# A layer norm, a long convolution and a feed-forward block on one core: x enters by (x - mean)(1 + rstd y) + mean, first writers write plainly, more transposes go by DMA, scales and first roots move to ScalarE

## The chip, the cores and the metric

The kernel runs on one core of a Trainium2 chip. The metric is the device time in microseconds, the median of several executions; lower is better. Separate executions of the kernel before lie between 1259.02 and 1259.97 us.

## What is computed

`x` has 2048 rows and 1024 columns, fp32. It is normalized by rows; the normalized rows gate a long causal convolution of `k` and `v`, and feed a feed-forward block of width 3584. Both results are added to `x`.

```python
def _A_ref(q, k, v, shift_k, ssm_k, ssm_D):      # q: the normalized x
    ...                                          # k_shift: four taps along the rows
    kv = k_shift * v
    kv_f, kf_f = rfft(kv, 2 * S), rfft(ssm_k, 2 * S)
    y = irfft(kv_f * kf_f)[:S] + kv * ssm_D
    return q * y

def _B_ref(x, w1, w2):
    return silu(x @ w1) @ w2

xn = (x - mean) / sqrt(var + 1e-5)
return x + _A_ref(xn, ...) + _B_ref(xn, B_w1, B_w2)
```

## The kernel before

One program issues all instructions in an order that a planner works out. Each piece of work is a generator that yields operations (`Op`: engine, estimated busy time, memory read and written) or conditions to wait for. `Order.run` keeps a clock for each engine and emits, again and again, the operation whose estimated start less its stream's bias is the earliest. Each engine then executes its own instructions strictly in the emitted order, and waits by semaphores where data or a buffer is not ready. `L` is a plain DMA issued from SyncE (SP), `X` a transposing DMA of 2-byte data from SP, `G` an accumulating DMA from GpSimd (POOL), `V`, `A` and `T` are VectorE, ScalarE and TensorE operations. Many operations pass through the same helpers: L348 and L351 (VectorE), L359 (ScalarE), L335, L341 and L345 (DMAs).

**Feed-forward.** Products are made of three fp16 matmuls (high and low parts), so each factor is split into a high part (ScalarE) and a low part (VectorE) with a scale that is a power of two. The scale comes from a sum of squares: `norm` adds it over partitions by a matmul with ones, and a chain on VectorE (reduce, a bound from below, two shifts that leave the exponent, then scalings by `then`) leaves it in `wsc` for the 14 column pairs of `w1`. `units` computes the first product by Strassen's seven products, on four PSUM banks `ff` that ScalarE and VectorE evacuate; `feed_forward` then computes the second product for the plain part of the width, row block by row block and half by half of the columns (`result`, ScalarE, scale `invc`), and `units2` the Strassen part. The hidden layer goes through device memory; its blocks come back into the twelve half buffers of `wo`. The parts of `w2` are split in `norms_w2`, in places that the first product leaves.

**Layer norm.** `ln_rows` takes rows in groups of 2, 2, 4 and 8 blocks: statistics on VectorE (two on ScalarE), then for each group a chain of eleven small VectorE instructions for the inverse root (L506 to L516), then the application to the rows (L528 on VectorE or ScalarE).

**Convolution.** Eight groups `g` of 128 channels, each in four steps `t`. `gate` makes k times v; its sums of squares give the group's scales in `csc` through `norm`. `signal_parts` transposes the signal and splits it: for `g < BY_DMA` (3) four TensorE transposes into a PSUM tile `py` and a split from there; for the other groups a split into the single buffer `cm` and two DMA transposes. `stage1`, `forward`, `product`, `inverse` and `stage1_inv` make the transform, the product and the inverse; `result_scales` makes the last scale by `norm` again. `norm_rows` loads x a second time in pieces `xg` and normalizes them on ScalarE; `gated` multiplies them by the convolution's result on VectorE (scalar `sc[:, 5:6]`) and adds them to `out` by POOL.

**Output.** `copies` first copies x to `out` by 16 DMAs of 512 KB on SP (L1161); everything else is added to it by accumulating DMAs on POOL: 64 half row blocks of the feed-forward and its Strassen part, and 64 pieces of the convolution. Only the very last piece is read back, added and written plainly.

Of the kernel before, what the change touches and what calls it, by code (L numbers as in the profile page):

```python
# [38 lines left out]
BY_DMA = 3  # L39
# [6 lines left out]
APPLY = (4, 5, 6, 7)  # L46
GUESS = 0x5f3759df
# [69 lines left out]
class Order:  # L117
# [4 lines left out]
    def __init__(self):  # L122
        self.free = defaultdict(float)
        self.wrote, self.read = {}, {}
        self.slots, self.patterns = {}, {}
        self.streams = []
        self.pipe = self.now = 0.0
        self.table = AF.Silu
# [171 lines left out]
def h3_ffn_kernel(ctx, tc, x, kp, vs, fs, shift, dskip, w1, w2, cfwd, cinv, out):  # L300
# [53 lines left out]
    def a_act(o, i, func, scale=1.0, bias=None, total=None):  # L354
        def f():
            kw = {} if bias is None else {"bias": bias}
            if total is not None:
                kw["accum_out"] = total
            nc.scalar.activation(o, i, func, scale=scale, **kw)  # L359
        ins = [i] + [s for s in (scale, bias) if s is not None and not isinstance(s, float)]  # L360
        p = A(f, o, ins)
        p.table = func if func == AF.Silu else None
# [22 lines left out]
    nmr = cst.tile([P, NT], F32, name="nmr")  # L385
    rstd = cst.tile([P, NT], F32, name="rstd")
# [9 lines left out]
    invc = cst.tile([P, 1], F32, name="invc")  # L396
    one = cst.tile([P, 1], F32, name="one")
# [40 lines left out]
    def norm(ring, ss, ns, then, flags, margin=1.5):  # L438
# [4 lines left out]
        e, etok = pw.tile([P, 2])  # L443
# [22 lines left out]
        for t in flags[1]:  # L466
            t.set()
# [11 lines left out]
    def ln_rows():  # L479
        for t0, n, bias in ((0, 2, 0.26), (2, 2, 0.17), (4, 4, LB), (8, 8, 0.03)):  # L480
# [36 lines left out]
            p = V(chain, r, [ag[:, 0:n]], us=1.8)  # L517
            p.writes += [e, f, v]
            yield p
            for k, t in enumerate(order_in):  # L520
                xt = xts[t][0]
                if k == (0 if t in APPLY else 1):
                    yield V(lambda: nc.vector.scalar_tensor_tensor(nmr[:, q], mean, -1.0, r, op0=MUL, op1=MUL), nmr[:, q], [ag[:, 0:n], r], us=0.2)
                if t in APPLY:
# [137 lines left out]
    def scales_w1():  # L662
        for n, (_, i) in enumerate(pairs):
# [19 lines left out]
            yield from norm(ctxs["nm"], ss[:, 0:m], (m,), then, ([wsc[:, i]], [flag["scaled", n], tok]))  # L683
# [288 lines left out]
    def feed_forward():  # L972
# [13 lines left out]
        for h in range(2):  # L986
            for ts in TOGETHER[h]:
                pos = {}
                for c in range(NC):
                    for t in ts:  # L990
# [11 lines left out]
                        if c == NC - 1:  # L1002
                            add(result(h, t, *pos[t]), EB)
                            flag["half"].set()
# [123 lines left out]
    flag["copied", 0] = Token(NT // 2)  # L1128
    flag["copied", 1] = Token(NT // 2)
    flag["conv out"] = Token(NG * 4 * 2)  # L1130

    def result(h, t, po, tok):
# [21 lines left out]

    def copies():
        for a in range(NT):
            yield flag["unit", a // 2] if a < NT // 2 else flag["half"]
            n = NT // 2
            q = slice(a % n * 2 * P, (a % n + 1) * 2 * P), slice(a // n * W, (a // n + 1) * W)
            o = out[q]  # L1160
            yield Op("SP", 0.4, 0.1, lambda: nc.sync.dma_start(o, x[q]), [], [], 0.3, P * D * 4)  # L1161
            flag["copied", a // n].set()
# [95 lines left out]
    def load_w2():  # L1258
        rings = ctxs["wraw"], ctxs["w2n"]
        for h, j in [(h, j) for h in range(2) for j in PLAIN[::2]]:  # L1260
            yield lambda: any(r.pairs() for r in rings)
            raw, tok = next(r for r in rings if r.pairs()).pair([P, 2, W])
            yield L(raw, w2r[:, j:j + 2, h * W:(h + 1) * W])
# [27 lines left out]
    def convolution(floor):  # L1291
# [19 lines left out]
        def rest(floor):  # L1311
# [8 lines left out]
            add(copies(), 0.0)  # L1320
# [28 lines left out]
        def gate():  # L1349

            for g in range(NG):
                yield csc_r.ready
                scs[g] = sc, _ = csc_r.tile([P, 8])
# [30 lines left out]
                def then(e):  # L1384
                    nc.vector.reciprocal(sc[:, 0:2], e)
                    nc.vector.tensor_scalar(sc[:, 0:2], sc[:, 0:2], 2.0 ** (15 - 64), None, op0=MUL)
                    nc.vector.tensor_scalar(sc[:, 2:4], e, 2.0 ** 64, None, op0=MUL)
                yield from norm(py_r, ss[:, 0:6], (4, 2), then, ([sc[:, 0:4]], [flag["scales", g]]), 4.0)
# [170 lines left out]
        def result_scales(g):  # L1559
# [4 lines left out]
            def then(e):  # L1564
                nc.vector.reciprocal(sc[:, 4:5], e)
                nc.vector.tensor_scalar(sc[:, 4:5], sc[:, 4:5], 2.0 ** (15 - 64 - 50), None, op0=MUL)
                nc.vector.scalar_tensor_tensor(sc[:, 5:6], e, 2.0 ** (64 - 41), sc[:, 2:3], op0=MUL, op1=MUL)
                nc.vector.tensor_tensor(sc[:, 5:6], sc[:, 5:6], sc[:, 3:4], op=MUL)
            yield from norm(py_r, ss[:, 8:12], (4,), then, ([sc[:, 4:6]], [flag["un", g], sss[g][1]]), 3.0)
# [54 lines left out]
        def norm_rows():  # L1624

            for g in range(NG):
                for t in TO:
# [33 lines left out]
        def gated(g, t, py, tok):  # L1661
# [4 lines left out]
            yield v_stt(flat[1], flat[0], sc[:, 5:6], flat[1], MUL, MUL)  # L1666
            tok.set()
            if t == TO[-1]:
                stok.set()
            yield flag["copied", g // (NG // 2)]  # L1670
            for b in range(2):
                yield G(out4[b][:, :, t, g * P:(g + 1) * P], xg[:, b])
                xtok.set()
                flag["conv out"].set()

# [24 lines left out]
    def more_rows():  # L1700
        for t in (8, 9, 12, 13, 10, 11, 14, 15):
            yield from load_row(t)
        yield L(taps, shift)
        yield L(cfw, cfwd)
        yield L(civ, cinv)

# [18 lines left out]
    nc.scalar.activation(warm, ones[:, 0:1], AF.Silu)  # L1725
# [56 lines left out]
```

## Time and profile before

| | before |
|---|---|
| median (lowest to highest of 3) | 1259.5 us (1259.02 to 1259.97) |
| profiled execution, its time | 1259.29 us |
| profiled execution, its span | 1257.5 us |
| mean granted TensorE clock | 0.996 |
| DMA, mean rate | 228 GB/s |

The profile shows one execution, instruction by instruction. A row of a group gives the line, engine and operation, what is written and read, the shapes and the count; then the busy time, the mean duration in ns, and the idle time of the engine just before these instructions with what ended it. A row of the timeline gives the start, the duration, the engine (PE is TensorE, PEld its weight loads, DVE VectorE, ACT ScalarE, POOL GpSimd; a q behind a name means its sequencer). A row of a window gives its length, the busy time of PE, PEld, DVE, ACT and POOL with the count of instructions, the granted clock, the busy share of the DMA engines and their GB/s. A row of waits gives who waited for whom, the sum in us, how often, and the longest. Matmuls are pipelined: their durations overlap, and their pitch is read from the starts.

### The profile page before, as it was taken

Reading aid. Unit: us, or ns where it says so; the run is one execution under the profiler, and the core shown is the slowest. Engines: PE = TensorE matmul, PEld = TensorE weight load, DVE = VectorE, ACT = ScalarE, POOL = GpSimd, SP = SyncE. Lnnn points to the kernel's source line nnn. Section 1 sums busy time; section 2 is a strip of 40 time slices with the busy share of each in tenths; the row PEclk is TensorE's granted clock in tenths of the full one; section 3 lists DMA queues with packets and bytes.
Section 4 is the critical chain, followed back from the end, with each engine's and each line's share of the span. In section 5 each row is a group of like instructions: output and inputs, shape, how many; then the busy total and the mean of one; then the engine's idle time right before and its main releaser. Section 6 shows DMA issues by size and latency. Waiting matters only on the chain. (4 is left out here: it accounts for less than half of the span.)

```text
span 1257.5 us, 17095 instructions
## 1 busy us (share of the span) xinstructions
PE 1234.0 (98%) x6066; PEld 600.4 (48%) x6066; DVE 1137.8 (90%) x1503; ACT 724.8 (58%) x1148; POOL 132.8 (11%) x141
## 2 busy tenths in 40 slices
PE   7999999999999999999999999999999999999997
PEld 6654444444444544444444544544544444454453
DVE  8999997997999979998999899899989989998961
ACT  7758887776677878568643632643453345552331
POOL 0000000000000110002000300300120120122241
PEclk8999999999999999999999999999999999999999
DMA  9097899889798899679997876789596498988784
GB/s 335 9 332 250 291 312 313 270 264 205 226 386 294 243 306 315 209 195 288 346 315 219 180 200 136 168 257 259 112 238 158 116 204 227 251 140 154 160 143 74
DMA packets 268309, 286.12 MB, mean 228 GB/s; under 512 B 65344, under 2 KB 184128, under 8 KB 266944
## 3 DMA queue, kind: packets, MB, share of 16 engines
q1 hardware_dynamic: 241488, 260.12, 66.8%
q0 software_dynamic: 26736, 24.92, 15.4%
q8 instruction: 47, 0.77, 0.3%
q14 instruction: 38, 0.31, 0.1%
HBM read 184.05 MB, written 96.73 MB: 223 GB/s over the span
## 5 line engine op out<-in xcount | busy, mean ns | idle before, releaser
L1016 PE MATMUL ff<-x,wo 128*128 128x512 f16 x864 | 327.4, 379 | 1.0 <-ACT hf L359 1.0
L1018 PE MATMUL ff<-x,wo 128*128 128x512 f16 x864 | 327.4, 379 | 0.0
L1017 PE MATMUL ff<-x,wo 128*128 128x512 f16 x864 | 327.4, 379 | 0.0
L887 PE MATMUL ff<-x,wo 128*128 128x512 f16 (+1 forms) x808 | 303.5, 376 | 3.9 <-ACT hf L359 2.6
L888 PE MATMUL ff<-x,wo 128*128 128x512 f16 (+1 forms) x808 | 303.5, 376 | 1.4 <-DVE x L351 1.4
L889 PE MATMUL ff<-x,wo 128*128 128x512 f16 (+1 forms) x808 | 303.5, 376 | 0.2 <-DVE wo L351 0.2
L348 DVE TENSOR_TENSOR spec<-spec 128x512 f32<-128x512 f32 (+2 forms) x256 | 261.5, 1052 | 2.4 <-DVE spec L348 0.5
L1018 PEld LDWEIGHTS <-wo 128*128 128x128 f16 x864 | 84.5, 98 | 102.0
L1016 PEld LDWEIGHTS <-wo 128*128 128x128 f16 x864 | 85.5, 99 | 98.8
L1017 PEld LDWEIGHTS <-wo 128*128 128x128 f16 x864 | 84.5, 98 | 100.5 <-issue 1.9
L889 PEld LDWEIGHTS <-wo 128*128 128x128 f16 x808 | 79.2, 98 | 94.6 <-issue 1.7
L888 PEld LDWEIGHTS <-wo 128*128 128x128 f16 x808 | 79.3, 98 | 92.1 <-issue 5.6
L887 PEld LDWEIGHTS <-wo 128*128 128x128 f16 x808 | 80.8, 100 | 86.9
L359 ACT ACTIVATE hf<-ff,invc 128x512 f32<-128x512 f32 x64 | 43.5, 679 | 114.1 <-PE ff L1018 106.5
L345 POOL DMA_DIRECT2D out<-hf x63 | 55.5, 881 | 495.4 <-ACT hf L359 426.6
L348 DVE TENSOR_TENSOR tmp<-spec 128x2048 f32<-128x2048 f32 (+1 forms) x48 | 92.3, 1930 | 0.7
L351 DVE SCALAR_TENSOR_TENSOR ht<-hf,wsc,ht 128x1024 f16<-128x1024 f32 (+1 forms) x56 | 67.2, 1201 | 7.3 <-ACT ht L359 7.2
L345 POOL DMA_DIRECT2D out<-xg x40 | 44.9, 1333 | 262.8 <-DVE hf L348 108.4
L359 ACT ACTIVATE spec<-ps 128x512 f32<-128x512 f32 x84 | 48.7, 591 | 36.8 <-PE ps L1464 35.9
L359 ACT ACTIVATE wo<-raw,wsc 128x512 f16<-128x512 f32 (+1 forms) x56 | 51.6, 927 | 27.6 <-DVE raw L348 14.8
L359 ACT ACTIVATE spec<-spec 128x1024 bf16<-128x1024 f32 x32 | 33.7, 1054 | 57.4 <-DVE spec L348 57.1
L351 DVE SCALAR_TENSOR_TENSOR acc<-kin,taps,acc 128x1024 f32<-128x1024 f32 x48 | 61.3, 1277 | 2.2 <-ACT acc L359 2.2
(171 smaller groups left out, 1769.6 us busy)
## 6 DMA issues: line engine op xcount, KB each, us to landing
wo<-hs SPq DMA_DIRECT2D x160, 256.0 KB, 4.0
hs<-ht SPq DMA_DIRECT2D x80, 256.0 KB, 5.2
out<-hf POOLq DMA_DIRECT2D x63, 256.0 KB, 4.4
raw<-in_w SPq DMA_DIRECT2D x28, 512.0 KB, 6.0
wraw<-in_w SPq DMA_DIRECT2D x24, 512.0 KB, 6.1
w2n<-in_w SPq DMA_DIRECT2D x24, 512.0 KB, 6.6
kin<-in_kp SPq DMA_DIRECT2D x16, 704.0 KB, 6.0
xt<-in_x SPq DMA_DIRECT2D x16, 512.0 KB, 7.5
```

The lines of the kernel that those rows point to most:

```text
L345: return Op("POOL", 1.1, 3.0, lambda: nc.gpsimd.dma_start(o, i, accum_op=ADD), [i], [o], m, 2.3 * n)
L348: return V(lambda: nc.vector.tensor_tensor(o, a, b, op=op), o, [a, b], **k)
L351: return V(lambda: nc.vector.scalar_tensor_tensor(o, a, s, b, op0=op0, op1=op1), o, [a, b] + ([] if isinstance(s, float) else [s]), **k)
L359: nc.scalar.activation(o, i, func, scale=scale, **kw)
L887: nc.tensor.matmul(o, w[:, 0, k], xf[:, :, k, 0], start=first and k == 0, stop=False, **kw)
L888: nc.tensor.matmul(o, w[:, 0, k], xf[:, :, k, 1], start=False, stop=False, **kw)
L889: nc.tensor.matmul(o, w[:, 1, k], xf[:, :, k, 0], start=False, stop=last and k == KH - 1, **kw)
L1016: nc.tensor.matmul(po, hx[:, n, 0, :], wc[:, n, 0, :], start=first and n == 0, stop=False, **kw)
L1017: nc.tensor.matmul(po, hx[:, n, 0, :], wc[:, n, 1, :], start=False, stop=False, **kw)
L1018: nc.tensor.matmul(po, hx[:, n, 1, :], wc[:, n, 0, :], start=False, stop=last and n == 3, **kw)
```

## The change

- **x.** The copies go. `norm_rows` now makes mean - x (scale -1, bias `mu`) instead of the normalized piece; `gated` first makes, with four ScalarE instructions in PSUM, `py` times a scalar per row (the inverse root times the group's negative scale) minus 1, and multiplies the two on VectorE: (x - mean)(1 + rstd y). `result` adds the mean as a bias.
- **Writes.** The first writer of each place of `out` writes plainly from SP: `result` for the first half (the two column halves change places, so these are columns 512 to 1023), and the convolution for the groups 0 to 3 (columns 0 to 511). The others accumulate from POOL, and wait for the first writer's flag.
- **Transposes.** `BY_DMA` goes from 3 to 1: groups 1 and 2 are transposed by DMA too.
- **Scales.** The norms of all groups and of the w1 pairs from the third on go through `norm_on_two`: sums on ScalarE with an accumulator, exponent and reciprocal on VectorE, the scalings by small ScalarE instructions.
- **Roots.** The first two groups of rows (t0 below `ROOTED`) take the root on ScalarE and a reciprocal on VectorE; the table loaded at the start is the root's, and Silu's is loaded later.
- **Loads.** `more_rows` loads the taps and the transform's constants ahead of the last four row blocks.

```diff
-BY_DMA = 3
+BY_DMA = 1
+ROOTED = 4
...
+    def small(o, i, scale, ins=()):
+        return Op("ACT", 0.2, 0.2, lambda: nc.scalar.activation(o, i, AF.Copy, scale=scale), [i, *ins], [o], 0.15)
+
+    def norm_on_two(ring, ss, ns, then, flags, margin=1.5):
+        yield ring.ready
+        pt, tok = ring.tile([P, W])
+        yield pw.ready
+        e, etok = pw.tile([P, 16])
+        cols, n = len(ns), sum(ns)
...
+        def halved():
+            a, r = e[:, 0:cols], e[:, 2:2 + cols]
+            nc.vector.tensor_scalar(a.bitcast(I32), a.bitcast(I32), 24, 23,
+                                    op0=ALU.logical_shift_right, op1=ALU.logical_shift_left)
+            nc.vector.reciprocal(r, a)
+
+        yield T(mm, pt[:, 0:n], [ss], 0.25, m=margin)
+        for c, m in enumerate(ns):
+            q = sum(ns[:c])
+            p = a_act(e[:, 8:8 + m], pt[:, q:q + m], AF.Identity, 1.0, tiny, total=e[:, c:c + 1])
+            p.busy = 0.4
+            yield p
+        tok.set()
+        yield V(halved, e[:, 0:4], [e[:, 0:2]], us=0.34)
+        yield from then(e[:, 0:cols], e[:, 2:2 + cols])
...
-            p = V(chain, r, [ag[:, 0:n]], us=1.8)
...
+            if t0 < ROOTED:
+                p = a_act(v, var, AF.Sqrt, 1.0, eps)
+                p.busy = 0.2
+                yield p
+                yield V(lambda: nc.vector.reciprocal(r, v), r, [v], us=0.18)
+            else:
...
     def result(h, t, po, tok):
...
-        yield a_act(o, po, AF.Copy, invc[:, 0:1])
+        yield a_act(o, po, AF.Identity, invc[:, 0:1], mu[:, t:t + 1])
         tok.set()
-        yield G(orr[t // T2, t % T2, :, h * W:(h + 1) * W], o)
+        to = orr[t // T2, t % T2, :, columns(h)]
+        if h == 0:
+            yield L(to, o)
+            flag["row", t].set()
+        else:
+            yield flag["conv row", t]
+            yield G(to, o)
...
-    def copies():
...
-                def then(e):
-                    nc.vector.reciprocal(sc[:, 0:2], e)
-                    nc.vector.tensor_scalar(sc[:, 0:2], sc[:, 0:2], 2.0 ** (15 - 64), None, op0=MUL)
-                    nc.vector.tensor_scalar(sc[:, 2:4], e, 2.0 ** 64, None, op0=MUL)
-                yield from norm(py_r, ss[:, 0:6], (4, 2), then, ([sc[:, 0:4]], [flag["scales", g]]), 4.0)
+                def scales(e, r):
+                    yield small(sc[:, 0:2], r, 2.0 ** (15 - 64))
+                    yield small(sc[:, 2:4], e, 2.0 ** 64)
+                    yield small(sc[:, 6:7], sc[:, 2:3], sc[:, 3:4], [sc[:, 3:4]])
+                yield from norm_on_two(py_r, ss[:, 0:6], (4, 2), scales, [flag["scales", g]], 4.0)
...
+            def scales(e, r):
+                yield small(sc[:, 4:5], r, 2.0 ** (15 - 64 - 50))
+                yield small(sc[:, 7:8], e, -2.0 ** (64 - 41))
+                yield small(sc[:, 5:6], sc[:, 7:8], sc[:, 6:7], [sc[:, 6:7]])
+                yield small(sc[:, 8:], rstd, sc[:, 5:6], [sc[:, 5:6]])
+            yield from norm_on_two(py_r, ss[:, 8:12], (4,), scales, [flag["un", g], sss[g][1]], 3.0)
...
-                            yield a_act(xg[:, b, i], xg[:, b, i], AF.Identity, rstd[:, n:n + 1], nmr[:, n:n + 1])
+                            yield a_act(xg[:, b, i], xg[:, b, i], AF.Identity, -1.0, mu[:, n:n + 1])
...
-            yield v_stt(flat[1], flat[0], sc[:, 5:6], flat[1], MUL, MUL)
-            tok.set()
+            rows = [[b * T2 + 4 * i + t for i in range(2)] for b in range(2)]
+            for b in range(2):
+                for i in range(2):
+                    k = 8 + rows[b][i]
+                    yield a_act(py[:, b, i], py[:, b, i], AF.Identity, sc[:, k:k + 1], minus)
...
-            yield flag["copied", g // (NG // 2)]
+            yield v_tt(flat[1], flat[0], flat[1], MUL)
+            tok.set()
             for b in range(2):
-                yield G(out4[b][:, :, t, g * P:(g + 1) * P], xg[:, b])
+                to = out4[b][:, :, t, g * P:(g + 1) * P]
+                if g < NG // 2:
+                    yield L(to, xg[:, b])
+                else:
+                    for n in rows[b]:
+                        yield flag["row", n]
+                    yield G(to, xg[:, b])
...
-    nc.scalar.activation(warm, ones[:, 0:1], AF.Silu)
+    nc.scalar.activation(warm, ones[:, 0:1], AF.Sqrt)
```

More of the change, by code (lines that the diff above doesn't have):

```diff
@@ L127, in __init__ @@
         self.pipe = self.now = 0.0
-        self.table = AF.Silu
+        self.table = AF.Sqrt
     def cells(self, a):
@@ L361, in a_act @@
         p = A(f, o, ins)
[L362 removed]
+        p.table = func if func in (AF.Silu, AF.Sqrt) else None
         p.busy += 0.07 * (len(ins) - 1) - 0.06 * (i.space == bass.MemoryType.PSUM)
@@ L466, in norm, with mm @@
         for t in flags[1]:
+            t.set()
+    def small(o, i, scale, ins=()):
[4 more added lines that the diff above has]
+        yield pw.ready
+        e, etok = pw.tile([P, 16])
+        cols, n = len(ns), sum(ns)
+        def mm():
+            nc.tensor.matmul(pt[:, 0:n], ones, ss, start=True, stop=True)
+        def halved():
[12 more added lines that the diff above has]
+        yield from then(e[:, 0:cols], e[:, 2:2 + cols])
+        etok.set()
+        for t in flags:
             t.set()
@@ L682, in then, with scales @@
                 nc.vector.tensor_scalar(sc[:, 0:3], powers[:, 0:3], e, None, op0=MUL)
-            yield from norm(ctxs["nm"], ss[:, 0:m], (m,), then, ([wsc[:, i]], [flag["scaled", n], tok]))
+            if n < 2:
+                yield from norm(ctxs["nm"], ss[:, 0:m], (m,), then, ([wsc[:, i]], [flag["scaled", n], tok]))
+                continue
+            def scales(e, r, i=i):
+                sc = wsc[:, i]
+                yield small(sc[:, 3:5], powers[:, 3:5], e, [e])
+                yield small(sc[:, 0:3], powers[:, 0:3], r, [r])
+            yield from norm_on_two(ctxs["nm"], ss[:, 0:m], (m,), scales, [flag["scaled", n], tok])
     spills = []
@@ L1705, in more_rows @@
         yield L(civ, cinv)
+        for t in (10, 11, 14, 15):
+            yield from load_row(t)
     def more_pairs():
```

46 lines of the change are left out of this document (22 added, 24 removed).

## The prediction

> **What bounds the kernel now.** I read the page's busy shares first, then the busy time by stage, then TensorE's own waits.
>
> ```profile
> span 1257.5 us, 17095 instructions
> PE 1234.0 (98%) x6066; PEld 600.4 (48%) x6066; DVE 1137.8 (90%) x1503; ACT 724.8 (58%) x1148; POOL 132.8 (11%) x141
> ...
> PEclk8999999999999999999999999999999999999999
> ```
> ```profile
> 0.00:30.00 30.00, 21.49 (x147) 18.37 (x148) 24.34 (x76) 21.36 (x47) 0.69 (x6) 0.89 0.98 349
> ...
> 400.00:500.00 100.00, 99.88 (x494) 48.39 (x493) 90.74 (x102) 80.22 (x135) 9.69 (x9) 1.00 0.92 279
> ...
> 1230.00:1258.00 28.00, 18.67 (x86) 8.22 (x84) 2.94 (x4) 4.02 (x6) 4.32 (x5) 0.94 0.45 71
> ```
> ```profile
> PE ft L547 <- DVE x L351: 3.8, 3, 2.1
> PE ft L547 <- DVE xt L528: 2.8, 2, 2.4
> PE ff L887 <- ACT hf L359: 2.6, 3, 1.4
> ...
> PE ps L1462 <- ACT tmp L359: 1.2, 2, 0.6
> ```
>
> TensorE is busy for 1234.0 of 1257.5 us at the full clock. Of its 23.5 us of idle time 8.5 lie in the first 30 us (30.00 - 21.49) and 8.8 behind 1230 (27.5 - 18.67); 6.2 are left for the 1200 us between. Its waits are for VectorE and ScalarE, none for a DMA. So there are three ways to a shorter time: less work on TensorE, an earlier start, fewer of those 6.2 us. An engine or a queue that merely gets lighter gives nothing, and ScalarE or VectorE can take time only by handing something to TensorE late. The profiled execution took 1259.29 us, its span and 1.8 us around it; that is 0.2 under the median of 1259.5, so sums are made from 1259.3.
>
> **Transposes on DMA from group 1 on.** Groups 1 and 2 of the convolution lose their four TensorE transposes per step, four steps each: 32 in eight bursts.
>
> ```profile
> 499.43 0.60 PE L1415 MATMUL py<-ident,acc 128*128 128x128 f32 x4
> 499.86 0.38 PE L887 MATMUL ff<-x,wo 128*128 128x512 f16 x1
> 500.08 0.38 PE L888 MATMUL ff<-x,wo 128*128 128x512 f16 x1
> ```
> ```profile
> L359 ACT ACTIVATE hi<-py,csc 128x512 f16<-128x512 f32 x12 | 8.2, 684 | 3.6 <-PE py L1415 1.8 <-PE ps L1464 1.4 <-DVE csc L1386 0.2
> ...
> L359 ACT ACTIVATE cm<-acc,csc 128x512 f16<-128x512 f32 x20 | 14.3, 715 | 20.5 <-DMA lo<-cm 11.6 <-DVE csc L1386 6.0 <-issue 2.9
> ```
> ```profile
> lo<-cm SPq DMA_TRANSPOSE x20, 3.7
> ```
>
> A burst holds TensorE from 499.43 to 499.86, 0.43 us, so 8 x 0.43 = **3.4 us** leave the engine that sets the end. By the group's other measure, 0.60 us of pipelined busy time, it would be 4.8; the next matmul starts at 0.43, so I take that. In its place come 8 splits into `cm` at 715 instead of 684 ns (0.2 us of ScalarE in all; VectorE's half is of the same form) and 16 DMA transposes of some 4 us. With one `cm` buffer the next split waits for the transposes, as groups 3 to 7 already do (11.6 us of ScalarE waiting over 20 splits), so about 0.6 x 8 = 5 us more of ScalarE waiting, in groups that lie beside the feed-forward matmuls. TensorE has waited for no DMA in the five groups that do it so: price 0, bounds 0 and +2 (one late part of 4 us in each of two groups, half of it covered).
>
> **Scales on ScalarE.** 28 norms move: 12 of w1, two for each of eight groups.
>
> ```profile
> 12.47 0.15 DVE L454 TENSOR_REDUCE pow<-nm 128x1 f32<-128x4 f32 x1
> ...
> 13.49 0.23 DVE L682 TENSOR_SCALAR wsc<-powers,pow 128x3 f32<-128x3 f32 x1
> ```
> ```profile
> L359 ACT ACTIVATION_READ_ACCUMULATOR junk<-x 128x1 f32 x8 | 1.5, 189 | 0.0
> ...
> L359 ACT ACTIVATE ag<-nt 128x1 f32<-128x1 f32 x4 | 0.8, 208 | 0.1
> ```
>
> On VectorE such a chain runs 12.47 to 13.72, 1.25 us; what stays is two short ones, about 0.4. That frees some 28 x 0.85 = 24 us. ScalarE gets, per norm, one or two sums (208 + 189 = 0.40 each) and two to four small scalings at 208: w1 0.82, group scales 2 x 0.40 + 3 x 0.21 = 1.4, result scales 0.40 + 4 x 0.21 = 1.2; together 12 x 0.82 + 8 x 2.6 = 31 us. The chain now crosses from PSUM to ScalarE, VectorE and back, so whatever is queued on ScalarE behind a small scaling waits for VectorE's `halved`; who waits for ScalarE then is TensorE, for banks.
>
> **x by (x-mean)(1+rstd y)+mean.**
>
> ```profile
> L359 ACT ACTIVATE xg<-xg,nmr,rstd 128x128 f32<-128x128 f32 x80 | 34.5, 482 | 14.5 <-DMA xg<-in_x 14.5
> ```
> ```profile
> 713.89 1.65 ACT L359 ACTIVATE xg<-xg,nmr,rstd 128x128 f32<-128x128 f32 x4 [1.51 <-DMA xg<-in_x]
> ```
> ```profile
> L351 DVE SCALAR_TENSOR_TENSOR xg<-py,csc,xg 128x512 f32<-128x512 f32 x20 | 14.9, 744 | 1.4 <-PE py L1655 1.4
> ```
>
> 32 steps get four new ScalarE instructions on `py`; the same size on `xg` takes 1.65 us for four, so 32 x 1.65 = 53 us. The four on `xg` lose one operand, the results gain a bias: small, opposite, left out. VectorE's `xg` of 744 ns becomes a plain product, at most a little shorter. ScalarE thus rises by 31 + 53 = 84 us to about 810, 64% of the span: no bound on average, but its windows decide.
>
> ```profile
> 560.00:580.00 20.00, 20.00 (x112) 10.81 (x110) 19.90 (x25) 16.00 (x26) 6.62 (x7) 1.00 0.88 205
> 580.00:600.00 20.00, 17.88 (x84) 7.93 (x82) 16.64 (x19) 17.95 (x28) 2.47 (x3) 1.00 1.12 337
> ```
>
> ScalarE has 33.95 of these 40 us, and TensorE already loses 2.1 here, to ScalarE. One group's gating and scales are 4 x 1.65 + 2.6 = 9.2 us; if they fall here, ScalarE has 43.2 for 40. Bounds 0 and +3.2; I take **+1.0**, because the lighter VectorE brings the group earlier. Against it stands that lighter VectorE itself: TensorE's waits of 6.2 in the middle hang on chains that pass it. It can give 0 to -3; I take **-1.0**.
>
> The Trainium skill speaks against this move: "ScalarE: Activation LUTs", section "Rules for kernel authors", sends adds, multiplies and maxima to VectorE. Here the small ones agree in direction (0.21 us on ScalarE, 0.15 to 0.23 on VectorE), yet the fuller engine is VectorE. By that rule the change would be a loss of the last rival's kind.
>
> **No copies, first writers plain.** The 16 copies of x leave, and 48 writes move from POOL's accumulating queue to SP: 16 results and 32 halves of the first four groups. No row has TensorE waiting for these transfers, so they are worth 0, and the price is on SP, which works in order:
>
> ```profile
> SPq L335 <- PE ff L1018: 291.1, 145, 4.8
> ```
>
> Behind a plain write that waits for ScalarE or VectorE stand loads of `wo`. SP spends 291.1 us waiting for TensorE to free just those buffers, twelve halves deep, so a write some us late is covered: 0. Without cover it would be one late load of about 4 us, once or twice. Taps and constants go ahead of the last four rows, before the stretch from 30 to 50 us in which the DMA engines are idle (0.02 and 0.07, quoted below): 0.
>
> **First roots.**
>
> ```profile
> 7.57 0.17 DVE L506 TENSOR_SCALAR nt<-ag 128x2 f32<-128x2 f32 x1
> ...
> 9.75 0.81 DVE L528 TENSOR_SCALAR xt<-xt,ag,rstd 128x1024 f32<-128x1024 f32 x1
> ...
> 20.16 0.17 DVE L506 TENSOR_SCALAR nt<-ag 128x2 f32<-128x2 f32 x1
> ...
> 22.34 0.81 DVE L528 TENSOR_SCALAR xt<-xt,ag,rstd 128x1024 f32<-128x1024 f32 x1
> ```
> ```profile
> 22.00:30.00 8.00, 5.27 (x44) 4.16 (x42) 7.75 (x21) 6.59 (x15) 0.00 (x0) 1.00 1.03 351
> 30.00:40.00 10.00, 10.00 (x70) 6.81 (x69) 9.24 (x32) 8.71 (x12) 0.00 (x0) 1.00 0.02 7
> 40.00:50.00 10.00, 9.26 (x58) 5.84 (x56) 10.00 (x17) 9.80 (x18) 0.00 (x0) 1.00 0.07 26
> ```
> ```profile
> 0.74 1.28 ACT L1725 ACT_TABLE_LOAD   x1 [0.74 <-PEq L1772]
> 2.03 0.20 ACT L1725 ACTIVATE warm<-one 128x1 f32<-128x1 f32 x1
> ```
>
> Two chains of 2.18 us on VectorE (7.57 to 9.75, 20.16 to 22.34) become a root of 0.21 on ScalarE and a reciprocal, taken like the chain's own steps at 0.17. ScalarE is in the middle of squares then, so the root can start up to about a microsecond late: each chain gains 0.6 to 1.7. TensorE waits here for just these rows (2.8 us) and what VectorE does after them (3.8), so the gain goes through; I take 1.25 each, 2.5. It is paid at the first Silu, where the table must change: 1.28 us by the row at the start, in 30 to 50 us, where two norms of w1 add 1.6. ScalarE has 18.51 of 20 there, so 2.9 more is 1.4 too much; I charge 1.0. **-1.5**, bounds -3.4 and +1.7 (1.2 gained, all 2.9 paid).
>
> The Trainium skill, "ScalarE: Activation LUTs", "What ACT_TABLE_LOAD costs", puts a drain of about 1.38 us beside the load's 1.28, 2.66 for a switch, and says to group calls by table set. The start shows a warm-up right behind the load, 2.03 against 0.74 + 1.28, but a first load has nothing to drain; by the page the sum is up to 1.4 us worse.
>
> **The tail.**
>
> ```profile
> 1249.06 0.38 PE L1018 MATMUL ff<-x,wo 128*128 128x512 f16 x1
> ```
>
> The last matmul ends at 1249.4; evacuations, an addition and writes fill the 8.1 us to 1257.5. They are not in the diff: 0.
>
> Sum: -3.4 - 1.5 + 1.0 - 1.0 = -4.9; 1259.3 - 4.9 = **1254.4 us**.
>
> **The rivals.**
>
> *Hidden after all: 1259.* TensorE arrives 3.4 us earlier at the second product, whose weights are split just in time.
>
> ```profile
> L1016 PE MATMUL ff<-x,wo x864: 376/379/379, 601.7 to 1248.6; 128*128 128x512 f16 x173
> ```
> ```profile
> 618.43 1.15 ACT L359 ACTIVATE x<-wraw,tau 128x1024 f16<-128x1024 f32 x1 [5.62 <-DMA wraw<-in_w]
> ```
> ```profile
> 621.98 1.27 DVE L351 SCALAR_TENSOR_TENSOR x<-w2n,tau,x 128x1024 f16<-128x1024 f32 x1
> ```
>
> The fifth block's last half is done at 623.25; TensorE needs it at about 623.6 (four blocks of 24 matmuls and a quarter of the fifth, from 601.7 on, at some 0.215 us each, 499.86 to 500.08). If these loads don't move up with TensorE, it gives 3.4 + 1.5 back or nearly: 1257 to 1262. For it: ScalarE waits 5.62 us for a load that is issued only when VectorE has freed its buffer. Against it: the first blocks need places that TensorE itself frees, and so move with it.
>
> *More than the sum: 1248.* Both roots gain in full (-3.4), no bank is late (0 for +1.0), the lighter VectorE takes 3 of the 6.2, and the removed bursts count 4.8: -11.2. For it: VectorE loses 30 us of 1138, and is at 90%. Against it: these waits are short and scattered, 5 us in 1200.
>
> *ScalarE becomes the bound in its full windows: 1264.* Its work in windows over 80% goes to TensorE: 2.9 in 30 to 50, 9.2 in 560 to 600, 9.2 in 400 to 500 (80.22 of 100) and some 5 of w1 norms before 200. Of these 26 us four tenths on TensorE are 10.4; with -3.4 and -2.5 it is +4.5, 1263.8. It decides from a quarter of them on (6.6 us against 5.9 gained). For it: TensorE's middle waits are for ScalarE, and 28 chains now make ScalarE wait for VectorE in order. Against it: a bank is evacuated while TensorE works on another product of 12 matmuls, 2.6 us, and ScalarE already waits for VectorE often, without a trace on TensorE.
>
> **How the numbers follow.** A measurement of this kernel tells 0.2% from no change, 2.5 us: faster is under 1257.0, slower over 1262.0. Forecast (1250.5 to 1257.0) 0.42, more than the sum 0.18, hidden 0.20, ScalarE's bound 0.20. So faster 0.60, same 0.20, slower 0.20. The range takes most of both outer cases: 1247 to 1264. The forecast's own range is 1250.5 to 1257.0.
>
> **What would show it.** Right: 16 transposes of `acc` on TensorE instead of 48 (busy sum some 4.8 lower), the first rows scaled about a microsecond before 9.75, one table load near 31 us, ScalarE near 810 us and VectorE near 1110, TensorE's middle waits still under 8. Wrong: waits of TensorE for `hf` or `ff` of ScalarE that grow by several us between 400 and 600 (third rival), a wait for `x<-wraw` or `x<-w2n` after 600 (first rival), any wait of TensorE for `lo<-cm`, more than two table loads, or a tail longer than 8 us behind the last matmul.

## The result, and the profile after

| | before | after |
|---|---|---|
| median (lowest to highest, 20 runs each) | 1259.12 us (1257.1 to 1262.35) | 1256.23 us (1254.17 to 1259.06) |
| ratio to before, 95% interval | | 0.9977 (0.997 to 0.9985) |
| profiled execution, its time | 1259.29 us | 1258.14 us |
| profiled execution, its span | 1257.5 us | 1256.4 us |

The change makes the kernel 2.9 us faster. The forecast was 1254.4, 4.9 us faster, with a range from 1247 to 1264. The profiled execution of after lies at the upper end of its own spread: its span is only 1.1 us shorter than that of before, and what follows is read from that one execution.

The page of after, span and busy time:

```profile
span 1256.4 us, 17146 instructions
PE 1232.6 (98%) x6034; PEld 597.5 (48%) x6034; DVE 1117.9 (89%) x1359; ACT 790.5 (63%) x1431; POOL 83.5 (7%) x93
```

ScalarE rose by 66 us (810 in all was expected; a part of the difference are the `xg` instructions, which without one operand take 390 ns instead of 482), VectorE fell by 20 (1110 was expected), POOL lost 49. The windows of after show where TensorE gains and loses:

```profile
0.00:30.00 30.00, 23.61 (x167) 20.30 (x168) 21.53 (x59) 21.34 (x47) 0.69 (x6) 0.89 0.97 367
...
560.00:580.00 20.00, 20.00 (x106) 10.28 (x105) 18.23 (x22) 18.84 (x31) 0.00 (x0) 1.00 0.89 272
580.00:600.00 20.00, 17.04 (x72) 7.30 (x71) 17.80 (x20) 16.04 (x28) 0.76 (x1) 0.91 1.08 328
1230.00:1258.00 28.00, 15.91 (x66) 6.53 (x64) 2.19 (x3) 2.75 (x4) 5.46 (x6) 0.86 0.45 71
```

In the first 30 us TensorE is busy for 2.1 us more than before (23.61 against 21.49). From 580 to 600 it has fewer matmuls (72 against 84) and a lower granted clock, 0.91 against 1.00. At 1230 it has 66 matmuls left where before had 86: at 0.215 us each it is 4.3 us ahead. That lead is near the predicted 4.9. Yet its last matmul, in the timeline of after, starts where it did before (1249.06):

```profile
1230.07 1.11 POOL L346 DMA_DIRECT2D out<-ht  x1 [3.27 <-issue]
1234.09 1.77 POOL L346 DMA_DIRECT2D out<-hf  x2 [2.91 <-issue]
1238.29 0.69 ACT L360 ACTIVATE hf<-ff,invc 128x512 f32<-128x512 f32 x1 [10.94 <-DMA out<-hf]
1239.03 0.38 PE L1074 MATMUL ff<-x,wo 128*128 128x512 f16 x1 [2.66 <-ACT hf L360]
...
1240.46 0.63 PE L1074 MATMUL ff<-x,wo 128*128 128x512 f16 x1
1240.89 0.63 PE L1075 MATMUL ff<-x,wo 128*128 128x512 f16 x1
...
1248.96 0.38 PE L1076 MATMUL ff<-x,wo 128*128 128x512 f16 x1
```

Read it from below. TensorE waits 2.66 us at 1239.03 for ScalarE to evacuate a bank. ScalarE waits 10.94 us for a buffer `hf`, and that buffer is held by an accumulating DMA that has not landed. POOL issues those DMAs in order, and each waits about 3 us, though POOL itself is idle: the last pieces of the convolution (`out<-ht`) and the feed-forward's last pieces (`out<-hf`) now stand mixed in its queue. Behind the gap the matmuls start 0.43 us apart instead of 0.215, each lasting 0.63: the clock is halved for about 3.4 us, which is another 1.7. Together the two make up the lead of 4.3. (A second wait of 0.78 us, at 1244.00, is no part of it: before has it too.)

### The profile page after: what moved, and what is told of

It is laid out like the page before. It is cut to its first block, busy times and chain, and to the rows that moved or that the text cites. A ratio compares the mean times of both kernels' runs of the same rounds, so it can differ in the third digit from the quotient of the medians.

```text
span 1256.4 us, 17146 instructions
## 1 busy us (share of the span) xinstructions
PE 1232.6 (98%) x6034; PEld 597.5 (48%) x6034; DVE 1117.9 (89%) x1359; ACT 790.5 (63%) x1431; POOL 83.5 (7%) x93
## 5 line engine op out<-in xcount | busy, mean ns | idle before, releaser
L360 ACT ACTIVATE spec<-ps 128x512 f32<-128x512 f32 x92 | 53.2, 592 | 28.7 <-PE ps L1522 28.0
L352 DVE SCALAR_TENSOR_TENSOR wo<-raw,wsc,wo 128x512 f16<-128x512 f32 (+1 forms) x56 | 56.4, 1012 | 11.9 <-ACT wo L360 11.9
L346 POOL DMA_DIRECT2D out<-hf x47 | 45.8, 981 | 303.9 <-ACT hf L360 254.4
L360 ACT ACTIVATE hf<-ff,invc 128x512 f32<-128x512 f32 x32 | 21.9, 684 | 65.7 <-PE ff L1076 47.6
L360 ACT ACTIVATE ht<-hf,wsc 128x1024 f16<-128x1024 f32 (+1 forms) x56 | 60.8, 1085 | 3.4 <-DVE hf L349 2.1
L349 DVE TENSOR_TENSOR spec<-tmp 128x512 f32<-128x512 f32 (+1 forms) x80 | 61.3, 792 | 0.7
```

The source lines that it names most:

```text
L346: return Op("POOL", 1.1, 3.0, lambda: nc.gpsimd.dma_start(o, i, accum_op=ADD), [i], [o], m, 2.3 * n)
L349: return V(lambda: nc.vector.tensor_tensor(o, a, b, op=op), o, [a, b], **k)
L352: return V(lambda: nc.vector.scalar_tensor_tensor(o, a, s, b, op0=op0, op1=op1), o, [a, b] + ([] if isinstance(s, float) else [s]), **k)
```

## The experiments

The executions of one kernel spread over 1.4 to 5.3 us and an interval on a ratio is 0.0015 to 0.0031 wide, so two kernels are told apart from about 3 us on. Microseconds between two kernels below are the difference of their ratios times 1259. A trace is one execution of each. One reserve holds for every part that is taken out or put in: the planner may then find another order. TensorE's sequence is the same in before and e2, and in after, e1 and e11; between e2 and e10 it differs from 428 us on. Runs that are compared with each other carry the same buffers for the tail, as said.

**Is it the tail that eats the lead? (e1, e2)** The last Strassen unit may put its pieces into the buffers of `w2`, free by then. e1 does that to after, e2 to before.

```diff
+        spare = [ctxs["wraw"], ctxs["w2n"]] if last else []
...
-            yield hfs.ready
-            o, otok = hfs.tile([P, W])
+            yield roomy
+            o, otok = out_tile()
```

> The changed kernel, but the last Strassen unit takes its evacuation buffers from the two idle w2 buffers instead of the hf ring, whose halves still wait for accumulating DMAs. Theory (TensorE is 4.3 us ahead at 1230 us and gives it back in the last unit, where ScalarE waits for a buffer held by an accumulating DMA, 2.66 us, and the clock drops after the gap): the wait for ScalarE in the last unit falls from 2.7 to below 0.9, the last matmul ends at about 1245, and the time falls by 3 to 6 us against the changed kernel, to 1250 to 1253. Rival (the end is set by the accumulating DMAs of the last group and the read behind them, whatever TensorE does): the last matmul moves up but the time stays within 1.5 us of 1256.

> The kernel before with the same other buffers in the last Strassen unit. Theory: before has no such gap in the last unit (its only gap there is 0.8 us), so TensorE ends as before at 1249; only the drain behind it, 8.1 us, shortens by the wait of the read for a buffer, 1 to 3 us: 1256 to 1258. Rival (the buffers alone are what a faster end needs, and the change gave nothing): as fast as the changed kernel with these buffers, within 1 us.

e1: 1252.39 us (1251.59 to 1255.18), ratio 0.9953 (0.9939 to 0.9966). e2: 1258.85 us, ratio 1.0002 (0.9992 to 1.0012). TensorE's waits and a stretch of the timeline of e1:

```profile
PE ff L946 <- ACT hf L360: 3.8, 2, 3.1
...
PE ff L1074 <- ACT w2n L360: 0.8, 1, 0.8
```
```profile
1242.30 0.33 SPq L336 DMA_DIRECT2D wraw<-out  x1
...
1244.75 0.38 PE L1076 MATMUL ff<-x,wo 128*128 128x512 f16 x1
1245.66 0.69 DVE L349 TENSOR_TENSOR wraw<-wraw 128x512 f32<-128x512 f32 x1 [5.14 <-DMA wraw<-out]
```

The wait of 2.66 is gone, the last matmul starts 4.2 us earlier than in after, and the time falls by 3.0 us. To before the same buffers give nothing: the 1 to 3 us that the drain was expected to lose were not lost (8.4 us in e2, 8.1 in before). So the change had made the tail's buffers the limit, and 3.0 us of its gain were lost there. What is left is the stall near 589 us (3.1), and behind the last matmul a read of `out` that is issued at 1242.30 and lands at 1245.66.

**The transposes alone (e3, e4, e5).** One line: e3 is after with `BY_DMA = 3`, e4 is before with `BY_DMA = 1`, e5 is e4 with the other tail buffers.

```diff
-BY_DMA = 3
+BY_DMA = 1
```

> The changed kernel with the transposes of groups 1 and 2 back on TensorE. Theory (each burst holds TensorE for 0.43 us, and its stream passes this on to the end): first matmul of the second product about 3.4 us later than 597.5 but for other gaps, time 1 to 4 us above the changed kernel, since its tail may take back a part. Rival (the DMA transposes cost as much as they save, or the gain is hidden): within 1 us of the changed kernel or faster.

> The kernel before with the transposes of groups 1 and 2 by DMA, nothing else. Theory: 2 to 4 us faster than before (3.4 on TensorE), no wait of TensorE for a DMA. Rival (without the removed copies the DMA engines are too full for 16 more transposes): the same or slower, with waits of TensorE or long landing times of the transposes, over 5 us.

> The kernel before with the transposes of groups 1 and 2 by DMA and with the w2 buffers in the last Strassen unit. Theory (the 3.4 us are won on TensorE, and without the other buffers lost in the last unit's wait for a buffer): 1255 to 1256.5, 2.5 to 4 us below the kernel before with these buffers (1258.85). Rival (the DMA transposes cost it elsewhere, in DMA or VectorE): within 1 us of 1258.85.

e3: 1257.76 us, ratio 0.999 (0.9981 to 0.9998). e4: 1260.12 us, 1.0011 (1.0002 to 1.002). e5: 1256.92 us, 0.9978 (0.9969 to 0.9987). The window and the timeline of e4:

```profile
1230.00:1258.00 28.00, 15.15 (x69) 6.53 (x67) 2.27 (x4) 2.75 (x4) 5.45 (x6) 0.89 0.45 71
```
```profile
1239.62 0.69 ACT L359 ACTIVATE hf<-ff,invc 128x512 f32<-128x512 f32 x1 [11.53 <-DMA out<-hf]
1240.36 0.38 PE L1016 MATMUL ff<-x,wo 128*128 128x512 f16 x1 [3.30 <-ACT hf L359]
```

e4 is the clearest case of the study: the one part whose price was surest makes TensorE 3.5 us earlier at 1230 (15.15 us of work left against 18.67), and the kernel no faster (by the ratio 1.4 us slower, with an interval from 0.3 to 2.5), because it runs into the same full buffers (3.30). Other buffers alone make it 4.2 us faster (e5 against e4). With them the transposes are worth 3.0 us (e5 against e2), and TensorE's busy sum falls from 1233.6 to 1229.8, by 3.8. e3 shows less, 1.6 us: it has no tail wait to begin with, and no stall near 586 us either (further down).

**The roots (e6).** e1 with the old chains and Silu's table from the start.

```diff
-ROOTED = 4
+ROOTED = 0
...
-        self.table = AF.Sqrt
+        self.table = AF.Silu
...
-    nc.scalar.activation(warm, ones[:, 0:1], AF.Sqrt)
+    nc.scalar.activation(warm, ones[:, 0:1], AF.Silu)
```

> The changed kernel with the w2 buffers in the last unit and all roots on VectorE again, Silu's table loaded at the start. Theory (the roots are an earlier start): TensorE's busy time in the first 30 us falls from 23.8 to about 21.5, one table load, and the time is 1 to 2.5 us above the 1252.4 with the roots. Rival (the table load between 29 and 30 us takes back what the roots bring): within 0.7 us of 1252.4.

e6: 1255.7 us (1253.2 to 1257.6), ratio 0.997 (0.9956 to 0.9984), 2.1 us over e1. The two intervals overlap, so the time doesn't settle it, and neither do the traces: without the roots TensorE makes 147 matmuls in the first 30 us (20.7 us of work; 21.5 was expected), with them 165, but at 1230 us the traced execution of e6 has 58 left and that of e1 66. The stall near 589 is 2.6 us in e6 and 3.1 in e1, and only in e1 does the clock halve behind it. The start of after shows what the roots do:

```profile
8.42 0.28 ACT L360 ACTIVATE nt<-ag,eps 128x2 f32<-128x2 f32 x1
8.93 0.81 DVE L579 TENSOR_SCALAR xt<-xt,ag,rstd 128x1024 f32<-128x1024 f32 x1
...
19.37 0.81 DVE L579 TENSOR_SCALAR xt<-xt,ag,rstd 128x1024 f32<-128x1024 f32 x1
...
29.01 1.28 ACT L360 ACT_TABLE_LOAD   x1
30.30 0.69 ACT L360 ACTIVATE hf<-ff,wsc 128x512 f32<-128x512 f32 x1
```

The rows are scaled at 8.93 and 19.37 instead of 9.75 and 22.34. The table is loaded once more, at 29.01, and the first Silu follows 1.29 us later.

**Scales and x, each without the other (e7, e8).** e7 is e1 with all norms back on VectorE. e8 has only the new form of x, with its plain writes, without copies and with the new load order: no roots, no scales on ScalarE, `BY_DMA = 3`.

```diff
-            yield from norm_on_two(py_r, ss[:, 8:12], (4,), scales, [flag["un", g], sss[g][1]], 3.0)
+            yield from norm(py_r, ss[:, 8:12], (4,), then, ([sc[:, 4:6], sc[:, 8:]], [flag["un", g], sss[g][1]]), 3.0)
```

> The changed kernel with the w2 buffers in the last unit and all scales on VectorE again, by the chains of before. Theory (VectorE's relief is worth about nothing to TensorE): within 1.5 us of 1252.4. First rival (the scalings on ScalarE are what makes it late at 586 us, where TensorE waits 3 us): that wait goes and the time is 2 to 4 us lower. Second rival (VectorE's relief is a gain): 2 us or more above 1252.4.

> Only the new form of x, the plain first writes, no copies and the order of the first loads, with the w2 buffers in the last unit: transposes, roots and scales as before. Theory (this part takes nothing from TensorE): within 1.2 us of 1258.85, the kernel before with these buffers. Rival (fewer accumulating DMAs and no copies let it run ahead): 2 us or more below. Other rival (four more instructions on ScalarE for each step make banks late): 2 us or more above.

e7: 1266.54 us, ratio 1.0059 (1.0046 to 1.0072), 13.3 us over e1. e8: 1268.48 us, ratio 1.0075 (1.006 to 1.0089), 9.2 us over e2. Neither is a small term. In e7 the wait of 3 us near 586 goes, as its first rival said, and the time rises all the same. The windows from 1200 to 1230 us, of before, e7 and e8 (the fourth number is VectorE's busy time):

```profile
1200.00:1230.00 30.00, 30.00 (x165) 15.89 (x164) 16.78 (x19) 8.40 (x10) 14.04 (x14) 1.00 0.88 136
```
```profile
1200.00:1230.00 30.00, 30.00 (x142) 13.75 (x141) 29.48 (x41) 10.42 (x15) 5.16 (x6) 1.00 0.64 136
```
```profile
1200.00:1230.00 30.00, 30.00 (x142) 13.79 (x141) 29.45 (x39) 9.75 (x16) 4.99 (x6) 1.00 0.63 124
```

In before, VectorE is done with the convolution about 1219 us and half idle in this window. With the new form of x and the scales still on VectorE it is full to 1230 and beyond: the last gating product ends at 1243 or 1244, so the convolution is more than 20 us late. TensorE is busy in the whole window; what it loses, it loses in many places before. Summed up to its last matmul it is idle for 23.2 us in e7 (1256.7 less the busy sum 1233.5) against 14.2 in e1.

**What in x makes the convolution late? (e9, e10)** e9 is e8 with the old load order. e10 is e2 with four more ScalarE instructions on the bank `py` ahead of each gating product, and nothing else of the change.

```diff
+            for b in range(2):
+                for i in range(2):
+                    yield a_act(py[:, b, i], py[:, b, i], AF.Identity, one[:, 0:1], zero)
             yield v_stt(flat[1], flat[0], sc[:, 5:6], flat[1], MUL, MUL)
```

> e8 (only the new form of x, with the writes, the load order and the other tail buffers) took 1268.5, 9.6 us over the kernel before with the same buffers. Here its load order alone is undone: taps and constants come behind all rows again. Theory A (the four gating instructions on ScalarE and the chain they lengthen make the convolution late): nothing changes, 1266 to 1270, VectorE still busy for more than 28 of the 30 us from 1200 to 1230, and the first group's factors still ready near 220 us. Theory B (the load order delays the first rows and with them the convolution's start): the first group is ready near 202 again and the time falls to 1258 to 1261.

> The kernel before with the other tail buffers (1258.85) and four more ScalarE instructions of 128x128 on the bank py (times 1 plus 0) ahead of each gating product; copies, writes, loads and all else as before. Theory A: these alone hold the bank and lengthen each group by enough to make the convolution late: 1264 to 1270, VectorE busy for 25 us or more from 1200 to 1230. Theory B (load order or plain writes are what costs): 1258 to 1260.5, VectorE at some 17 us there.

e9: 1266.73 us, ratio 1.0053 (1.004 to 1.0065). e10: 1272.09 us, ratio 1.0094 (1.0079 to 1.011). The same window, of e9 and of e10:

```profile
1200.00:1230.00 30.00, 30.00 (x166) 16.06 (x164) 22.65 (x34) 14.69 (x26) 10.57 (x11) 1.00 0.77 146
```
```profile
1200.00:1230.00 30.00, 30.00 (x154) 14.87 (x152) 27.01 (x35) 10.83 (x17) 5.65 (x7) 1.00 0.75 158
```

The four instructions, with the order that the planner makes with them, cost 11.6 us (e10 against e2), more than the whole new form in e8. So they are enough to explain the cost. The load order is not: without it the new form still costs 6.4 us (e9 against e2), and its removal gives 2.8 at most (the intervals of e8 and e9 just overlap). Theory A's time for e9 was right, its two signs were not: the first load into `kf` starts at 203.8 us (220.5 in e8, 202.1 in e2), and VectorE has 22.65 us of work in the window, not 28. So the load order does delay the convolution, and little of that reaches the time. e10 lies above the 1270 named.

How the cost arises isn't shown. A late convolution is not its measure: the last gating product ends at 1221.0 us in e2, 1229.4 in e9, 1240.2 in e10 and 1243.9 in e8, while the times lie 6.4, 11.6 and 9.2 us over e2; e12 below has it at 1209.7 and is slower than e1. What the traces do show is TensorE's idle time up to its last matmul: 17.3 us in e2, 26.0 in e10, in waits of at most 2.1 us; from 1000 to 1200 us it is 4.5 in e10 and 0.3 in e2. The group of the new instructions in after:

```profile
L360 ACT ACTIVATE py<-py,minus,csc 128x128 f32<-128x128 f32 x96 | 40.7, 430 | 8.0 <-PE py L1713 6.3
...
L360 ACT ACTIVATE xg<-xg,mu 128x128 f32<-128x128 f32 x80 | 26.5, 390 | 10.8 <-DMA xg<-in_x 9.3 <-DVE spec L349 1.5
```

They take 430 ns each (32 more stand in an `ff` bank). Four of them are 1.7 us ahead of VectorE's product on one bank, in a chain in which that product of 0.75 us stood alone.

**The tail once more (e11).** e1, and the read of `out` for the last piece is issued at the start of the last unit, into a buffer of its own.

```diff
+        if last:
+            yield flag["conv out"]
+            yield ctxs["w2n"].ready
+            o, otok = ctxs["w2n"].tile([P, W])
+            yield L(o, at(u, 1, 0))
         yield ff.ready
```

> The changed kernel with the other tail buffers (e1, 1252.4), and the read of out for the very last piece issued at the start of the last unit, into a buffer of its own. In e1 the last matmul ends at 1245.2 and the span at 1253.3; the read is issued at 1242.3 and landed at 1245.7, behind the last matmul. Theory (this read ends the drain): the drain shrinks from 8.2 to 4.5 to 6 us, 1249 to 1251. Rival (the writes of the last pieces and their landing end it): 1252 to 1253, drain over 7.5.

e11: 1249.21 us (1248.35 to 1250.68), ratio 0.9914 (0.9902 to 0.9927), the best of all. The timeline of e11:

```profile
1242.58 0.38 PE L1076 MATMUL ff<-x,wo 128*128 128x512 f16 x1
1243.00 0.75 DVE L352 SCALAR_TENSOR_TENSOR wraw<-ff,invc,wraw 128x512 f32<-128x512 f32 x1 [4.05 <-PE ff L1076]
1243.77 0.34 SPq L336 DMA_DIRECT2D out<-wraw  x1
```

From the end of the last matmul (1242.96) to the end of the span (1247.9) are 4.9 us; in e1 they were 8.2. So the read did end the drain. The other 2 us between the two traces lie ahead of it, in places that the edit doesn't touch: 0.8 us of idle time in the first 30 us and 1.2 from 580 to 600. TensorE's sequence is the same in both, so that part may be spread between executions.

**x undone in the whole (e12).** e1 with x as before: copies, accumulating writes, normalized pieces, no gating on ScalarE, old load order. Only transposes, scales and roots are new.

```diff
-                    yield a_act(py[:, b, i], py[:, b, i], AF.Identity, sc[:, k:k + 1], minus)
...
-            yield v_tt(flat[1], flat[0], flat[1], MUL)
+            yield v_stt(flat[1], flat[0], sc[:, 5:6], flat[1], MUL, MUL)
+            tok.set()
...
+            add(copies(), 0.0)
```

> Transposes by DMA, roots and scales of the change with the other tail buffers; x as before (copies, accumulating writes, normalized pieces, no gating on ScalarE, old load order). Compared with e1 (1252.4) it tells what the form of x costs when VectorE has been relieved. Theory (the lighter VectorE covers most of the 9 us that it costs alone, and what is left is the stall of 3 us near 586 us, where ScalarE is at the gating): 1248.5 to 1251, no single wait over 2 us in the middle. Rival 1 (covered fully, the stall is someone else's): 1252 to 1253. Rival 2 (scales give the rest of their 13 us only when x needs it, and leaving the copies away is a gain of its own): over 1254.

e12: 1263.4 us (1261.91 to 1264.53), ratio 1.0028 (1.0018 to 1.0037): 9.4 us slower than e1. The expectation failed on the side of its second rival. Its timeline:

```profile
583.87 0.58 PE L1524 MATMUL ps<-lo,cfw 128*128 128x512 f16 x1 [2.14 <-DMA lo<-cm]
584.25 0.63 PE L1525 MATMUL ps<-hi,cfw 128*128 128x512 f16 x1
...
624.64 1.15 ACT L360 ACTIVATE x<-w2n,tau 128x1024 f16<-128x1024 f32 x1 [0.52 <-DMA w2n<-in_w]
625.84 0.38 PE L1070 MATMUL ff<-x,wo 128*128 128x512 f16 x1 [2.52 <-ACT x L360]
626.61 1.28 DVE L352 SCALAR_TENSOR_TENSOR x<-w2n,tau,x 128x1024 f16<-128x1024 f32 x1
627.94 0.59 PE L1071 MATMUL ff<-x,wo 128*128 128x512 f16 x1 [1.73 <-DVE x L352]
```

Here the prediction's first rival happens at its place: TensorE stands 4.2 us between 623 and 628 for the split parts of `w2`, and the clock is halved behind it. VectorE's split that is ready at 627.89 was ready at 623.25 before. The first wait, 2.14, is for a DMA transpose. With TensorE's idle time between 1000 and 1200 us 1.6 us longer than in e1, its last matmul comes 9.4 us later. VectorE is nearly idle after 1209, so the convolution is early here; that was no help. And against e5, which has the transposes and these buffers only, roots and scales cost 6.3 us here: the same scales whose return to VectorE costs 13.3 us where x has its new form (e7). Why `w2` is split so late without the new x was not tried further: copies, the load order and the planner's whole order change together.

## Why the prediction was right, and where it was not

The direction held, and 1256.2 lies in the forecast's own range (1250.5 to 1257.0), at its upper end. One term was right, one right in kind, and one zero, the tail, was wrong by 3.0 us. The other two were wrong in mechanism and by about ten times in size, and that they cancel is luck: with the tail repaired the change gains 6.2 us (e1 against e2), of which transposes and roots are some 5.1, so new x and scales together come out near the zero that was forecast.

**Transposes, -3.4:** right. 3.0 us by e5 against e2, 3.8 us of TensorE's busy sum; no DMA stands among the waits of TensorE in after (in e12 one does, 2.14 us for `lo<-cm`). The count of `acc` transposes on TensorE fell as named:

```profile
L1473 PE MATMUL py<-ident,acc 128*128 128x128 f32 x16 | 2.2, 273 | 0.0
```

**Roots, -1.5:** right in kind, not settled in size. 2.1 us by the ratios, with intervals that overlap. The gain per chain was 0.8 and 3.0 against the 1.25 taken, the second helped by an earlier first; the price was one table load of 1.28. The Trainium skill, "ScalarE: Activation LUTs", "What ACT_TABLE_LOAD costs", adds a drain of 1.38 us to a switch, and by it the first Silu would have come no sooner than 31.7; this trace has it at 30.30, so no drain shows here.

**ScalarE's full windows, +1.0, and a lighter VectorE, -1.0:** the step that failed. Both were priced by what TensorE might wait in one window of 40 us. The runs show that the new form of x costs 9.2 us where VectorE keeps its scales, and that moving the scales is worth 13.3 us where the new form is there. The premise that fell is the sentence that an engine which merely gets lighter gives nothing: VectorE's 90% was read as slack. The opposite is no rule either, since the same relief, with the roots, costs 6.3 us where x is as before (e12 against e5). What failed is the pricing of each move by itself: what one is worth depends on the other. Four instructions of ScalarE in the convolution's chain cost 11.6 us (e10); by which waits, and how much of it by the planner's other order, stays open. The rule of the Trainium skill, to use VectorE for multiplies ("ScalarE: Activation LUTs", "Rules for kernel authors"), applied to the scales would have given 1266.5 by e7, so it doesn't hold for this change as a whole; with the old x, e12 and e5 point the other way.

**"At the full clock"** overlooks the first 30 us, where the quoted row has 0.89. It changed nothing: TensorE makes 147 matmuls there at 0.89 (before), at 0.94 (e4) and at 1.00 (e6), since it waits for rows.

**No copies, plain writes, 0:** not isolated. e12 shows that going back to the old x, copies included, costs 9.4 us in the presence of the rest. Which part of it is the copies stays open.

**The tail, 0:** wrong. "They are not in the diff" is no reason: the writes that POOL issues there are, and a TensorE that comes 4.3 us earlier meets buffers that come free no earlier. e1 gives 3.0 us back, e4 shows the same with the transposes alone. The drain behind the last matmul did stay under the named bound (7.0 us against 8), so the sign that was to show a wrong tail looked at the wrong place; the wait lies ahead of the last matmul.

**The third rival** (ScalarE bound, 1264) was right about the place. The wait and the stretch of ScalarE ahead of it, in the timeline of after:

```profile
583.97 1.15 ACT L360 ACTIVATE x<-w2n,tau 128x1024 f16<-128x1024 f32 x1 [1.19 <-DMA w2n<-in_w]
585.02 1.80 ACT L360 ACTIVATE py<-py,minus,csc 128x128 f32<-128x128 f32 x4
586.75 0.71 ACT L360 ACTIVATE hi<-kf,csc 128x512 f16<-128x512 f32 x1
587.37 0.58 ACT L360 ACTIVATE hf<-ff 128x512 f32<-128x512 f32 x1
588.00 0.40 PE L946 MATMUL ff<-x,wo 128*128 128x512 f16 x1 [2.96 <-ACT hf L360]
588.22 0.61 PE L947 MATMUL ff<-x,wo 128*128 128x512 f16 x1
```

TensorE waits 2.96 us for an evacuation that stands behind the gating, and the halved clock takes 1.7 more. Before lost 2.1 in this stage. So the window cost some 2.6 us, between the +1.0 taken and the bound of 3.2. That the gating is its cause isn't shown, and three runs speak against the gating alone. e12 has none, and TensorE is idle there for 4.1 us from 580 to 600 all the same. e3 (transposes back on TensorE) and e7 (scales back on VectorE) have the gating, and lose 1.0 us and nothing there, the second with 1.1 us lost just before:

```profile
580.00:600.00 20.00, 19.04 (x89) 8.46 (x88) 16.57 (x19) 18.89 (x29) 0.00 (x0) 1.00 1.00 312
```
```profile
580.00:600.00 20.00, 20.00 (x112) 10.84 (x111) 19.49 (x22) 19.08 (x32) 0.00 (x0) 1.00 1.05 287
```

**The first rival** (weights of `w2` late) didn't happen in after and did in e12; it was the right thing to watch.

## What to carry to other kernels

A part that is surely worth 3 us on the bounding engine can measure as a loss, if what comes behind it has no room for an earlier arrival (e4): before a term is summed, look who frees the buffers at the very end, and when. Parts of a change that load and relieve the same engines are to be priced together, and measured together as well as apart: the new x alone costs 9.2 us (e8 against e2), the rest without it 3.3 (e12 against e2), and together, with the tail repaired, they gain 6.2 (e1 against e2). A busy share of 90% says neither that there is slack nor that relief will help. And where a planner orders the instructions, a part that is taken out takes the order with it: its price holds for that order.

## What the runs showed of the hardware

- The granted clock changes on a grid of 3.41 us, and what halves it is the idle time of TensorE within one such stretch, not the length of a wait. In after the wait of 2.96 us falls into one stretch, and the next has half the clock (0.50); in e4 the longer wait of 3.30 us is divided between two stretches (1.38 and 1.92 us), and the clock stays (rows below). In all traces here, a stretch at full clock with 2.0 us or more of idle time was followed by half the clock, one with 1.7 or less never was, and in between both occur. In a stretch at half the clock matmuls last 0.63 us and start 0.43 apart, so it costs up to 1.7 us. The grid lies elsewhere in each execution, so the same wait may or may not cost it: waits of 2.55 (e6) and 2.34 us (e5) did not. The Trainium skill, "TensorE: Matmul & The Clock Gate", "What's actually happening", gives the same window, 3413 ns that run freely, and ties the drop to an idle window; here a partly idle one was enough.
- A switch of the activation table cost 1.28 us, without a further delay ahead of the next activation (29.01 to 30.30 in after).
- Accumulating DMAs at the end come from POOL about 4 us apart (1230.07, 1234.09) while POOL is idle for 3 us before each. By the code, accumulations onto the same places wait for each other to land; that this is the whole of the 3 us isn't shown.

The stretches of the first point, of after (the wait ends at 588.00) and of e4 (it ends at 1240.36):

```profile
581.40:584.81 3.41, 3.41 (x17) 1.57 (x16) 3.41 (x3) 2.22 (x4) 0.00 (x0) 1.00 1.15 245
584.81:588.22 3.41, 0.45 (x4) 0.10 (x2) 2.77 (x5) 3.31 (x8) 0.00 (x0) 1.00 1.15 343
588.22:591.64 3.42, 3.42 (x10) 1.22 (x9) 3.39 (x4) 1.86 (x6) 0.00 (x0) 0.50 1.06 325
```
```profile
1235.02:1238.44 3.42, 2.04 (x10) 0.81 (x9) 0.00 (x0) 0.00 (x0) 1.76 (x2) 1.00 0.48 60
1238.44:1241.85 3.41, 1.50 (x7) 0.68 (x7) 0.00 (x0) 0.86 (x2) 0.00 (x0) 1.00 0.64 94
1241.85:1245.26 3.41, 2.63 (x13) 1.16 (x12) 0.75 (x1) 1.20 (x2) 1.20 (x2) 1.00 0.35 36
```
